# Attention and two MoE layers on one core: a planner that keeps VectorE's two-operand SBUF work and GpSimd's work apart

## The chip, the core and the metric

The kernel runs on one core of a Trainium2 chip. The metric is device time in microseconds (us) of one execution, the median of the runs shown. The core's engines are TensorE (PE in the rows, PEld for its weight loads), VectorE (DVE), ScalarE (ACT), GpSimd (POOL) and SyncE (SP, which issues the transfers). Each engine takes its instructions strictly in the order in which the program holds them. They wait for one another through semaphores.

## The reference

```python
def _attn_ref(q, k, v, tau):                  # q, k, v: (4, 8, 576, 64) fp32
    scores = np.matmul(q, k.transpose(0, 1, 3, 2)) / np.sqrt(64)
    thresh = np.max(scores, axis=-1, keepdims=True) - tau
    scores = np.where(scores >= thresh, scores, -1e9)
    attn = np.exp(scores - np.max(scores, axis=-1, keepdims=True))
    attn = attn / (np.sum(attn, axis=-1, keepdims=True) + 1e-9)
    return np.matmul(attn, v)
# x: (2304, 512); w_in: (512, 2048); w_out: (2048, 512)
def _moe_ref(x, w_in, w_out):
    h = x @ w_in
    return (h * np.tanh(softplus(h))) @ w_out
def _moe2_ref(x, w_in, w_out):
    h = x @ w_in
    return (h * np.clip(h + 3.0, 0.0, 6.0) / 6.0) @ w_out
# out = _moe2_ref(_moe_ref(attention, first pair of weights), second pair)
```

(`softplus` stands here for the reference's log1p form.)

## The kernel before

**Attention.** Heads are taken in 16 pairs. The 576 queries of a pair are four tiles of 128 and one of 64. Per pair, `k` and `q` are split into a high and a low fp32r part and `v` into two fp16 parts: ScalarE makes the high parts, VectorE the low parts of `k` (`kl`, line 982) and `v` (`vl`, line 1003), and GpSimd or VectorE the low part of `q` (`ql`). For a tile and a head the steps are: scores on TensorE into one of two PSUM buffers (`s`, line 1045), the row maximum on VectorE (`pk`, 1054), the exponential on ScalarE (`ex`, 1064), the threshold (`th`, 1059), the mask on VectorE (`mk`, 1067, the rows `e_ex<-s_s,...`), the fp16 high part on ScalarE (`ph`, 1072), the low part on GpSimd (`pl`, 317, two instructions `p_ph<-e_ex,p_ph`), a transposing transfer (`tr`), and the product with `v` on TensorE (`pv`, 1093). A score buffer is free again only when the mask has read it.

**Weights.** The four weight matrices arrive as 64-bit words, eight groups each. For a group VectorE takes a maximum (374) and some small scale instructions, ScalarE rescales the high words (490), GpSimd or VectorE shifts two halves left (`c`, 498 on GpSimd, 500 on VectorE), VectorE merges sign and low bits in two steps over 128x1024 words (506 and 511, called c3 and c4 here), ScalarE makes the fp16 high part (516), and GpSimd or VectorE the two halves of the low part (317, `w<-cvt_...`). After the eighth group a run of small VectorE instructions makes the scales (`zs`, 407 to 425). The first matrix is converted at the start of attention, the second at its end, the other two while the first dense layer runs.

**Dense layers.** The first product of the first layer (`h_g`, 648) is interleaved with attention. After attention come its activation and second product (`y_y`, 812), then the second layer (648 and 824), in which TensorE has nearly no idle time.

**What sets the order.** All of this is put into a `Plan` as tasks with a due time, engines that may take them with a cost each, dependencies and buffers. `Plan.run` goes forward with one clock per engine: of all open tasks it takes the one that can start first (within a small window per engine the one due first), puts its instructions at the end of that engine's queue, and moves that engine's clock by the cost. So costs and clocks decide the order on each engine, and at times the engine; on the chip only that order is left. In `_start` a task that GpSimd could take as well is started on VectorE 0.75 us late (`SLOW`). GpSimd's clock and VectorE's know nothing of each other.

Of the kernel before, what the change touches and what calls it, by code (L numbers as in the profile page):

```python
# [55 lines left out]
FLIP = 1.61  # L56
ALPHA = {"act": 3.07, "pe": 10.98}
FITS = 0.09
CRIT = ("s", "pk", "ex", "mk", "th")
BACKLOG = 99.0  # L60
MERGE_HI = False
# [67 lines left out]
class Plan:  # L129
# [10 lines left out]
    def __init__(self):  # L140
        self.clock = dict.fromkeys(("pe", "dve", "act", "pool", "sp"), 0.0)
        self.dma = 0.0
        self.warm, self.window, self.used = False, 1, 0.0
        self.open = {e: [] for e in self.clock}
        self.left = 0

# [25 lines left out]
    def _start(self, task, e):  # L172
        t = task.ready[e]
        for b in task.bufs:
            if b.slot is None:
                w = b.ring.when()
                if w is None:
                    return None
                t = max(t, w)
        if e == "sp" and not task.name.startswith("tr"):  # L180
            t = max(t + SLACK, self.dma - BACKLOG)
        if e == "dve" and len(task.engines) > 1:
            return max(t, self.clock[e]) + SLOW
        return max(t, self.clock[e])
# [43 lines left out]
    def run(self, until=None):  # L228
        while self.left and (until is None or any(t.end is None for t in until)):
# [18 lines left out]
            if e == "dve" and len(task.engines) > 1:  # L248
                start = max(start - SLOW, self.clock[e])
            cost = task.engines[e]  # L250
            if e == "pe":
                cost = self._clocked(start, cost, 0.75 if task.kind == "s" else 1.0)
            end = start + cost
            self.clock[e] = end
            if e == "sp":
                self.dma = max(self.dma, end + 1.1) + task.dma
                if task.kind == "tr":
                    self.clock[e] = max(end, self.dma - 0.95)
                end = self.dma + 1.1
            task.end = end  # L260
            task.fn(e)
            for b in task.bufs:
                b.drop(end)
            self.left -= 1
# [7 lines left out]
def fused_kernel(ctx: ExitStack, tc, q, k, v, tau, w1i, w1o, w2i, w2o, out):  # L272
# [125 lines left out]
    def summary(task, m, after):  # L398
# [25 lines left out]
            ts(w["c"][:, 0:1], w["c"][:, 0:1], 2.0 ** 10, None, ALU.mult)  # L424
            ts(w["f"], w["is"], w["c"][:, 1:2], None, ALU.mult)

        return task({"dve": 2.2 if n > 1 else 0.6}, scales, after, [], f"zs{m}")

    def tasker(at):
        def task(engines, fn, deps, bufs, tag, dma=0.0):  # L430
# [49 lines left out]
    def one_conversion(m, g, raw, deps, task):  # L480
# [37 lines left out]
        def lo(e, j):  # L518
            sub(e, dst[:, j, 1], t.tile[:, j].bitcast(F32), dst[:, j, 0])

        a = task(EXPAND, c1, deps, [raw, t], "c" + nm)
        b = [task(SHIFT, lambda e, j=j: c2(e, j), [a], [t], f"c{nm}{j}") for j in range(2)]
        a = task({"dve": 1.6}, c3, b, [raw, t], "c" + nm)
        a = task({"dve": 1.6}, c4, [a], [raw, t], "c" + nm)
        a = task({"act": 1.05}, hi, [a], [t], "h" + nm)
        for j in range(2):
            converted[m, 2 * g + j] = task(
                {"pool": 1.35, "dve": 0.68}, lambda e, j=j: lo(e, j), [a], [t], f"o{nm}{j}"
            )

    def split(task, name, src, sv, dst, inverse, ring, deps):
# [178 lines left out]
    def outer(ph, blk, x=None, ready=None):  # L710
# [30 lines left out]
        for fp in range(NG):  # L741
# [55 lines left out]
            a = chain["gs"] = task(  # L797
                {"act": 0.63}, hi, [a, scaled], [g, s], f"h{fp}", 0.0, fp, [chain["gs"]]
            )
            cost = {"dve": 0.75} if ph == 0 else {"pool": 1.35, "dve": 0.68}  # L800
            made.append(task(cost, lo, [a], [g, s], f"o{fp}", 0.0, fp))

        y = Buf(r_y)

# [153 lines left out]
    def pair(n, begin, values, sets):  # L958
# [4 lines left out]
        def prep(engines, fn, deps, bufs, tag, dma=0.0, at=early, order=()):  # L963
            return add(engines, fn, deps, bufs, at, 0.0, dma, f"{tag}{n}", order)
# [29 lines left out]
        a = prep({"act": 1.155}, lambda e: q_hi(slice(0, 2)), [lq], [rq, qs], "qh")  # L994
        for j in range(2):
            ql.append(prep(both(S), lambda e, j=j: q_lo(e, j), [a], [rq, qs], f"ql{j}_"))
        kl = prep({"dve": 1.8}, k_lo, [kh], [rk, kd, kld], "kl")

        def v_hi(e):
            nc.scalar.activation(vh.tile[:, :, :, :D], vb.tile, AF.Copy, scale=vs.tile)  # L1000
# [6 lines left out]
        def vprep(engines, fn, deps, bufs, tag):  # L1007
            return prep(engines, fn, [deps], bufs, tag, 0.0, base)

        a = vprep({"act": 0.83}, v_hi, scaled, [vb, vs, vh], "vh")  # L1010
        split = vprep({"dve": 1.3}, v_lo, a, [vb, vs, vh, vl], "vl")

        def query_tiles(t, c, o, i):
            at = START + t * STEP
# [246 lines left out]
    t = 0  # L1261
# [133 lines left out]
```

## Time and profile before

| | |
|---|---|
| median of 3 runs (1112.82 to 1121.19) | 1114.16 us |
| the profiled execution: its time, its span | 1116.12 us, 1114.3 us |
| busy: TensorE, VectorE, ScalarE, GpSimd | 980.6, 641.4, 610.2, 471.1 us |
| instructions: TensorE, VectorE, GpSimd | 8839, 1069, 397 |
| mean granted TensorE clock (share of 2.4 GHz) | 0.952 |

Times in rows are microseconds from the start of the span unless marked ns. A busy time runs from an instruction's start to its end, so that an instruction which started and was then held up by another engine counts as busy all that time. The rows of a line whose instructions do the same work show this: their shortest is the work, the rest is waiting inside the instruction.

### The profile page before, as it was taken

Reading aid. Unit: us, or ns where it says so; the run is one execution under the profiler, and the core shown is the slowest. Engines: PE = TensorE matmul, PEld = TensorE weight load, DVE = VectorE, ACT = ScalarE, POOL = GpSimd, SP = SyncE. Lnnn points to the kernel's source line nnn. Section 1 sums busy time; section 2 is a strip of 40 time slices with the busy share of each in tenths; the row PEclk is TensorE's granted clock in tenths of the full one; section 3 lists DMA queues with packets and bytes.
Section 4 is the critical chain, followed back from the end, with each engine's and each line's share of the span. In section 5 each row is a group of like instructions: output and inputs, shape, how many; then the busy total and the mean of one; then the engine's idle time right before and its main releaser. Section 6 shows DMA issues by size and latency. Waiting matters only on the chain. (4 is left out here: it accounts for less than half of the span.)

```text
span 1114.3 us, 21604 instructions
## 1 busy us (share of the span) xinstructions
PE 980.6 (88%) x8839; PEld 795.1 (71%) x8839; DVE 641.4 (58%) x1069; ACT 610.2 (55%) x992; POOL 471.1 (42%) x397
## 2 busy tenths in 40 slices
PE   2356698997999896879998999899999999999997
PEld 2256587986988785868887888787666666676663
DVE  7998998777777778767788788632111111111110
ACT  6565687886787776646665576632323323323322
POOL 4887665664565657543433045321212212212211
PEclk9977698997999996899999999999999999999999
DMA  8877379999799997765655986401100100100001
GB/s 274 211 211 189 86 208 239 193 238 232 155 217 194 199 218 166 164 236 214 228 191 196 346 309 239 141 21 38 39 11 29 38 12 28 39 16 24 19 1 38
DMA packets 199394, 162.87 MB, mean 146 GB/s; under 512 B 174080, under 2 KB 174080, under 8 KB 194176
## 3 DMA queue, kind: packets, MB, share of 16 engines
q1 hardware_dynamic: 199296, 161.51, 53.3%
q8 instruction: 69, 1.13, 0.4%
q14 instruction: 29, 0.24, 0.1%
HBM read 90.18 MB, written 28.84 MB: 107 GB/s over the span
## 5 line engine op out<-in xcount | busy, mean ns | idle before, releaser
L648 PEld LDWEIGHTS <-w 128*128 128x128 f16 x3456 | 335.0, 99 | 71.8 <-issue 10.6
L317 POOL TENSOR_TENSOR p_ph<-e_ex,p_ph 128x128 f16<-128x128 f32 (+3 forms) x160 | 194.4, 1236 | 128.0 <-ACT p_ph L1072 66.1
L317 POOL TENSOR_TENSOR gs_h<-hl_r,gs_h 128x512 f16<-128x512 f32 x72 | 83.2, 1156 | 302.1 <-ACT gs_h L787 302.1
L824 PE MATMUL y_y<-w,gs_h 128*128 128x512 f16 x864 | 201.2, 379 | 0.0
L812 PE MATMUL y_y<-gs_h,w 128*128 128x256 f16 x1728 | 192.3, 273 | 7.7 <-DVE yl_zhy L552 3.3
L648 PE MATMUL h_g<-x_fl,w 128*128 128x256 f16 x1536 | 189.5, 278 | 8.4 <-ACT he_t L696 6.4
L812 PEld LDWEIGHTS <-w 128*128 128x128 f16 x1728 | 168.3, 98 | 27.7 <-issue 8.2
L824 PEld LDWEIGHTS <-gs_h 128*128 128x128 f16 x864 | 84.5, 98 | 82.8
L787 ACT ACTIVATE gs_h<-hl_r 128x512 f16<-128x512 f32 x72 | 45.3, 629 | 159.1 <-PE y_y L824 155.3
L1054 DVE TENSOR_REDUCE nm_pk<-s_s 128x1 f32<-128x576 f32 x144 | 106.2, 752 | 40.7 <-PE s_s L1045 40.3
L1064 ACT ACTIVATE e_ex<-s_s,nm_pk 128x576 f32<-128x576 f32 x144 | 104.2, 731 | 29.9 <-DVE nm_pk L1054 25.1
L771 DVE SCALAR_TENSOR_TENSOR hl_r<-hl_r,f,hp_g 128x512 f32<-128x512 f32 x36 | 26.9, 747 | 161.8 <-ACT hl_r L765 161.8
L1067 DVE SCALAR_TENSOR_TENSOR e_ex<-s_s,thr_th,e_ex 128x576 f32<-128x576 f32 x144 | 111.6, 810 | 13.1 <-ACT thr_th L1059 10.6
L1093 PE MATMUL aux_pv<-vh,pt_tr 128*128 128x65 f16 (+1 forms) x1296 | 95.0, 212 | 18.8 <-DMA pt_tr<-p_ph 18.7
L1072 ACT ACTIVATE p_ph<-e_ex 128x576 f16<-128x576 f32 x144 | 95.7, 680 | 23.7 <-DVE e_ex L1067 22.0
L1045 PE MATMUL s_s<-kda_kh,qs 128*128 128x288 f32 x200 | 72.9, 377 | 39.8 <-DVE e_ex L1067 24.2
L1093 PEld LDWEIGHTS <-pt_tr 128*128 128x128 f16 x2016 | 88.9, 108 | 25.4 <-DMA pt_tr<-p_ph 23.4
L771 DVE SCALAR_TENSOR_TENSOR hl_r<-hl_r,f,h_g 128x512 f32<-128x512 f32 x36 | 26.9, 747 | 137.5 <-ACT hl_r L765 137.5
L648 PE MATMUL h_g<-xl_x,w 128*128 128x256 f16 x864 | 103.5, 273 | 0.0
L648 PE MATMUL hp_g<-xl_x,w 128*128 128x256 f16 x864 | 103.1, 273 | 0.0
L1045 PEld LDWEIGHTS s_s<-kda_kh,qs 128*128 128x128 f32 x200 | 46.1, 231 | 55.9 <-issue 29.6
L1045 PE MATMUL s_s<-klda_kl,qs 128*128 128x288 f32 x200 | 65.7, 341 | 0.0
(331 smaller groups left out, 1335.7 us busy)
## 6 DMA issues: line engine op xcount, KB each, us to landing
hd<-he_t SPq DMA_DIRECT2D x36, 512.0 KB, 3.7
hl_l<-hd SPq DMA_DIRECT2D x36, 512.0 KB, 5.1
raw_lr<-in_moe_w_in SPq DMA_DIRECT2D x16, 1024.0 KB, 5.9
raw_lr<-in_moe_w_out SPq DMA_DIRECT2D x16, 1024.0 KB, 7.2
rk_lk<-in_k SPq DMA_DIRECT2D x16, 576.0 KB, 4.9
rq_lq<-in_q SPq DMA_DIRECT2D x16, 576.0 KB, 5.9
raw_lw<-in_moe_w_out SPq DMA_DIRECT2D x8, 1024.0 KB, 7.3
v_lv<-in_v SPq DMA_DIRECT2D x16, 320.0 KB, 4.2
```

The costliest lines, as they stand in the source:

```text
L317: engine[e].tensor_tensor(dst, a, b, ALU.subtract)
L648: mm(hv[:, j, :], wj[:, wl, c * P : (c + 1) * P], x.tile[:, c, xl, :], start=j == 0 and n == 0, stop=j == 1 and n == 11, skip_group_check= ...
L771: nc.vector.scalar_tensor_tensor(half(g), half(g), wsc[2]["f"][:, fp : fp + 1], h.tile, ALU.min, ALU.mult)
L787: nc.scalar.activation(s.tile[:, 0], gv(), AF.Copy)
L812: mm(yv[:, h, :], wt[m2][f // 2][:, f % 2, wl, c * P : (c + 1) * P], gs[fp].tile[:, gl, f % 2, :], start=fp == 0 and n == 0, stop=fp == NG ...
L824: mm(y.tile[:, j], gs[fp].tile[:, gl, f % 2, j * P : (j + 1) * P], wt[m2][f // 2][:, f % 2, wl, :], start=fp == 0 and n == 0, stop=fp == N ...
L1045: mm(s[j].tile[:, half, :HALF], lh, rh[:, half * HALF : (half + 1) * HALF], start=m == 0, stop=m == len(terms) - 1,)
L1054: nc.vector.tensor_reduce(neg.tile[:, j : j + 1], sv(j), AX.XY, ALU.max, negate=True)
L1064: nc.scalar.activation(ev(j), sv(j), AF.Exp, bias=neg.tile[:, j : j + 1])
L1067: nc.vector.scalar_tensor_tensor(ev(j), sv(j), thr.tile[:, j : j + 1], ev(j), ALU.is_ge, ALU.mult)
L1072: nc.scalar.activation(p16.tile[:, js, :S], e_.tile[:, js], AF.Copy)
L1093: mm(ov[:, dst, :d], pt.tile[:, j, ch, :], part.tile[:, src, vc, :], start=i == j == ch == 0 and part is vh, stop=j == w - 1 and ch == 8, ...
```

## The change

The planner now makes two kinds of task exclude each other. A VectorE task whose kind is in `PORT` starts no earlier than GpSimd's clock, and a GpSimd task no earlier than the end of the last such VectorE task. The kinds are the low parts of `k`, `v`, `q` and of the weights, the shifts and merges of the weights, and the scale runs. The costs of these tasks, which were means with some waiting in them, become lower. A tag is renamed where the low part reads PSUM (`n`), so that it isn't in `PORT`, and where it belongs to a weight (`u`). `give` stays `None` everywhere, so `YIELD` is added nowhere. No instruction is given another form, and no semaphore is added: what changes is the order on each engine, and the engine of some halves.

```diff
+PORT = ("kl", "vl", "c", "ql", "u", "o", "zs")
+YIELD = 0.1
...
+        self.port, self.give = 0.0, None
...
+        if e == "dve" and task.kind in PORT:
+            t = max(t, self.clock["pool"])
+        if e == "pool":
+            t = max(t, self.port)
         if e == "dve" and len(task.engines) > 1:
             return max(t, self.clock[e]) + SLOW
...
             cost = task.engines[e]
+            if e == "pool" and self.give:
+                cost += YIELD
...
             self.clock[e] = end
+            if e == "dve" and task.kind in PORT:
+                self.port = end
...
             task.fn(e)
+            if e == "pool" and self.give:
+                self.give()
...
-        return task({"dve": 2.2 if n > 1 else 0.6}, scales, after, [], f"zs{m}")
+        return task({"dve": 1.6 if n > 1 else 0.6}, scales, after, [], f"zs{m}")
...
-        a = task({"dve": 1.6}, c3, b, [raw, t], "c" + nm)
-        a = task({"dve": 1.6}, c4, [a], [raw, t], "c" + nm)
+        a = task({"dve": 1.22}, c3, b, [raw, t], "c" + nm)
+        a = task({"dve": 1.22}, c4, [a], [raw, t], "c" + nm)
...
-                {"pool": 1.35, "dve": 0.68}, lambda e, j=j: lo(e, j), [a], [t], f"o{nm}{j}"
+                {"pool": 1.25, "dve": 0.68}, lambda e, j=j: lo(e, j), [a], [t], f"u{nm}{j}"
...
-            cost = {"dve": 0.75} if ph == 0 else {"pool": 1.35, "dve": 0.68}
-            made.append(task(cost, lo, [a], [g, s], f"o{fp}", 0.0, fp))
+            cost, tag = ({"dve": 0.75}, "n") if ph == 0 else ({"pool": 1.25, "dve": 0.68}, "o")
+            made.append(task(cost, lo, [a], [g, s], f"{tag}{fp}", 0.0, fp))
...
-        kl = prep({"dve": 1.8}, k_lo, [kh], [rk, kd, kld], "kl")
+        kl = prep({"dve": 1.42}, k_lo, [kh], [rk, kd, kld], "kl")
...
-        split = vprep({"dve": 1.3}, v_lo, a, [vb, vs, vh, vl], "vl")
+        split = vprep({"dve": 0.88}, v_lo, a, [vb, vs, vh, vl], "vl")
```

**Place one: VectorE in the first tiles, around a low part of `v` (`vlb_vl`).** Before, the fourth pair's stood between the row maxima (`nm_pk`) and both masks (`e_ex`) of a tile:

```order
L1054 TENSOR_REDUCE nm_pk_1_0_1_414<-s_s_1_1_0_375 128x1
L1164 TENSOR_SCALAR den_dt_0_2_429<-aux_pv_0_0_1_314 128x4
L1003 SCALAR_TENSOR_TENSOR vlb_vl_3_431<-v_lv_0_0_169,vs_ve_1_184,vh_140 128x640
L1067 SCALAR_TENSOR_TENSOR e_ex_1_0_2_421<-s_s_1_0_0_364,thr_th_1_0_1_433,e_ex_1_0_2_421 128x576
L1067 SCALAR_TENSOR_TENSOR e_ex_1_0_2_421<-s_s_1_1_0_375,thr_th_1_0_1_433,e_ex_1_0_2_421 128x576
L982 SCALAR_TENSOR_TENSOR kldb_kl_2_449<-rk_lk_0_369,qscale,kdb_kh_1_438 128x1152
L506 SCALAR_TENSOR_TENSOR cvt_c_1__1_424<-raw_lr_1_0_177,cvt_c_1__1_424 128x1024
```

Now the third pair's stands two tiles later than before, behind a merge (524 is the old 511) and ahead of the second row maximum of its tile:

```order
L1067 TENSOR_REDUCE nm_pk_0_0_1_446<-s_s_0_0_0_437 128x1
L524 SCALAR_TENSOR_TENSOR cvt_c_0__1_281<-raw_lr_0_0_175,cvt_c_0__1_281 128x1024
L1016 SCALAR_TENSOR_TENSOR vlb_vl_3_459<-v_lv_0_0_167,vs_ve_1_184,vh_136 128x640
L1067 TENSOR_REDUCE nm_pk_0_0_1_446<-s_s_0_1_0_448 128x1
L330 TENSOR_TENSOR x_fl_0_2_430<-aux_fl_0_1_429,x_fl_0_2_430 128x256
L1080 SCALAR_TENSOR_TENSOR e_ex_0_0_2_457<-s_s_0_0_0_437,thr_th_0_0_1_499,e_ex_0_0_2_457 128x576
L1080 SCALAR_TENSOR_TENSOR e_ex_0_0_2_457<-s_s_0_1_0_448,thr_th_0_0_1_499,e_ex_0_0_2_457 128x576
```

**Place two: VectorE between the twelfth and the thirteenth mask.** Before, no more than 16 instructions stood between two masks anywhere in the first conversion. The third group's merges stood like this:

```order
L1067 SCALAR_TENSOR_TENSOR e_ex_1_0_2_556<-s_s_1_1_0_508,thr_th_1_0_1_559,e_ex_1_0_2_556 128x576
L317 TENSOR_TENSOR x_fl_0_2_523<-aux_fl_0_1_522,x_fl_0_2_523 128x256
L506 SCALAR_TENSOR_TENSOR cvt_c_2__1_520<-raw_lr_2_0_416,cvt_c_2__1_520 128x1024
L385 TENSOR_SCALAR top_146<-top_146 128x1
L511 SCALAR_TENSOR_TENSOR cvt_c_2__1_520<-raw_lr_2_0_416,cvt_c_2__1_520 128x1024
L1054 TENSOR_REDUCE nm_pk_0_0_1_620<-s_s_0_0_0_599 128x1
```

Now 33 instructions stand between these two masks, and in their middle five that are in `PORT` follow one another:

```order
L330 TENSOR_TENSOR x_fl_0_2_430<-aux_fl_0_1_590,x_fl_0_2_430 128x256
L524 SCALAR_TENSOR_TENSOR cvt_c_1__1_412<-raw_lr_1_0_177,cvt_c_1__1_412 128x1024
L519 SCALAR_TENSOR_TENSOR cvt_c_2__1_588<-raw_lr_2_0_491,cvt_c_2__1_588 128x1024
L995 SCALAR_TENSOR_TENSOR kldb_kl_2_633<-rk_lk_0_375,qscale,kdb_kh_1_433 128x1152
L524 SCALAR_TENSOR_TENSOR cvt_c_2__1_588<-raw_lr_2_0_491,cvt_c_2__1_588 128x1024
L1016 SCALAR_TENSOR_TENSOR vlb_vl_3_671<-v_lv_0_0_169,vs_ve_1_184,vh_140 128x640
L1177 TENSOR_SCALAR den_dt_0_2_676<-aux_pv_0_0_1_593 128x4
L1067 TENSOR_REDUCE nm_pk_0_0_1_679<-s_s_0_0_0_666 128x1
```

Two groups' merges and the preparation of two pairs have moved together, with no mask between them.

**Place three: GpSimd in the conversion of the second matrix.** Before, one of the two shifts of the third and of the fourth group stood on VectorE, and GpSimd had the other:

```order
L498 TENSOR_TENSOR cvt_c_2__1_6586<-cvt_c_2__1_6586,eight 128x512
L317 TENSOR_TENSOR p_ph_4_0_1_6634<-e_ex_4_0_2_6604,p_ph_4_0_1_6634 128x64
L317 TENSOR_TENSOR p_ph_4_0_1_6634<-e_ex_4_0_2_6604,p_ph_4_0_1_6634 128x512
L317 TENSOR_TENSOR w_2_5416<-cvt_c_2__1_6586,w_2_5416 128x512 x2
L498 TENSOR_TENSOR cvt_c_3__1_6748<-cvt_c_3__1_6748,eight 128x512
L317 TENSOR_TENSOR w_3_5417<-cvt_c_3__1_6748,w_3_5417 128x512 x2
```

Now GpSimd has both halves (511 is the old 498), as of every group of every matrix:

```order
L330 TENSOR_TENSOR p_ph_4_0_1_6609<-e_ex_4_0_2_6584,p_ph_4_0_1_6609 128x64
L330 TENSOR_TENSOR p_ph_4_0_1_6609<-e_ex_4_0_2_6584,p_ph_4_0_1_6609 128x512
L511 TENSOR_TENSOR cvt_c_2__1_6635<-cvt_c_2__1_6635,eight 128x512 x2
L511 TENSOR_TENSOR cvt_c_3__1_6732<-cvt_c_3__1_6732,eight 128x512 x2
L330 TENSOR_TENSOR w_2_5431<-cvt_c_2__1_6635,w_2_5431 128x512 x2
L330 TENSOR_TENSOR w_3_5432<-cvt_c_3__1_6732,w_3_5432 128x512 x2
```

Six shifts and five low parts have moved in this way from VectorE to GpSimd in the whole program. In return VectorE takes six more of the evacuations that ScalarE shares with it (`he_t`), and four small normalisations of tail rows.

## Rows read from the trace of the kernel before

**Rows 1.** The page's first part: busy time of each engine, share, instructions.
```profile
PE 980.6 (88%) x8839; PEld 795.1 (71%) x8839; DVE 641.4 (58%) x1069; ACT 610.2 (55%) x992; POOL 471.1 (42%) x397
```
**Rows 2.** Windows: stretch, length, busy of PE, PEld, DVE, ACT, POOL, clock, DMA.
```profile
10.00:150.00 140.00, 78.97 (x687) 69.68 (x688) 128.78 (x196) 91.02 (x145) 105.01 (x80) 0.83 0.71 192
150.00:480.00 330.00, 290.29 (x3418) 262.27 (x3417) 258.14 (x438) 249.85 (x451) 191.19 (x159) 0.92 0.92 203
480.00:712.00 232.00, 214.71 (x1952) 190.62 (x1950) 184.29 (x320) 148.82 (x223) 90.18 (x71) 0.99 0.66 234
712.00:1115.00 403.00, 396.35 (x2786) 272.41 (x2785) 65.52 (x103) 118.07 (x174) 83.21 (x72) 1.00 0.09 30
```
**Rows 3.** Waits of PE, 0 to 712 us: total, times, longest.
```profile
PE s_s L1045 <- DVE e_ex L1067: 40.4, 22, 7.1
PE aux_pv L1093 <- DMA pt_tr<-p_ph: 18.7, 15, 2.5
PE h_zp L348 <- DVE he_t L698: 4.6, 1, 4.6
```
**Rows 4.** Timeline of DVE from 38.9 us: start, duration, instruction.
```profile
39.00 5.69 DVE L1003 SCALAR_TENSOR_TENSOR vlb_vl<-v_lv,vs_ve,vh 128x640 f16<-128x640 f32 x1
44.61 1.53 DVE L1067 SCALAR_TENSOR_TENSOR e_ex<-s_s,thr_th,e_ex 128x576 f32<-128x576 f32 x2
```
**Rows 5.** Timeline of POOL from 38 us.
```profile
38.28 2.51 POOL L317 TENSOR_TENSOR p_ph<-e_ex,p_ph 128x128 f16<-128x128 f32 x2
40.75 2.25 POOL L317 TENSOR_TENSOR w<-cvt_c__1_282,w 128x512 f16<-128x512 f32 x2
42.98 2.61 POOL L498 TENSOR_TENSOR cvt_c__1_424<-cvt_c__1_424,eight 128x512 int32<-128x512 int32 x2
```
**Rows 6.** Timeline of PE at 45 us, with the idle time before.
```profile
45.56 0.58 PE L1045 MATMUL s_s<-kdb_kh,qs 128*128 128x288 f32 x1 [7.13 <-DVE e_ex L1067]
```
**Rows 7.** Windows of line 1003 alone (`vl`): stretch, length, DVE busy, clock, DMA.
```profile
0.00:180.00 180.00, 18.02 (x8) 0.85 0.75 201
```
**Rows 8.** Line 1003 to 180 us: ns shortest/median/longest, first and last start.
```profile
L1003 DVE SCALAR_TENSOR_TENSOR vla_vl<-v_lv,vs_ve,vh x4: 873/1172/2234, 12.5 to 150.0; 128x640 f16<-128x640 f32 x4
```
**Rows 9.** Windows of line 982 alone (`kl`).
```profile
0.00:180.00 180.00, 13.97 (x8) 0.85 0.75 201
```
**Rows 10.** Line 982 to 180 us, as in Rows 8.
```profile
L982 DVE SCALAR_TENSOR_TENSOR klda_kl<-rk_lk,qscale,kda_kh x4: 1406/1418/2268, 10.5 to 136.5; 128x1152 fp32r<-128x1152 f32 x4
```
**Rows 11.** Windows of line 506 alone (c3).
```profile
0.00:180.00 180.00, 12.52 (x8) 0.85 0.75 201
```
**Rows 12.** Windows of line 511 alone (c4).
```profile
0.00:180.00 180.00, 15.19 (x8) 0.85 0.75 201
```
**Rows 13.** Line 511 to 180 us, one of its eight.
```profile
L511 DVE SCALAR_TENSOR_TENSOR cvt_c__1_802<-raw_lr,cvt_c__1_802 x1: 1211/1211/1211, 89.2 to 89.2; 128x1024 uint32<-128x1024 uint32 x1
```
**Rows 14.** Timeline of DVE from 123.5 us, the scale run (`zs`).
```profile
123.57 2.03 DVE L407 TENSOR_SCALAR s<-sc 128x8 f32<-128x8 f32 x1
125.63 5.54 DVE L408 TENSOR_SCALAR s<-s 128x8 uint32<-128x8 uint32 x1
131.21 0.17 DVE L409 TENSOR_SCALAR is<-s 128x8 uint32<-128x8 uint32 x1
```
**Rows 15.** Timeline of POOL, two places: a `ql`, and two shifts.
```profile
25.16 1.41 POOL L317 TENSOR_TENSOR qs<-rq_lq,qs 64x576 fp32r<-64x576 f32 x1
...
59.35 2.06 POOL L498 TENSOR_TENSOR cvt_c__1_520<-cvt_c__1_520,eight 128x512 int32<-128x512 int32 x2
```
**Rows 16.** Lines of DVE to 180 us: count, busy, mean ns, idle before.
```profile
L1054 DVE TENSOR_REDUCE nm_pk<-s_s 128x1 f32<-128x576 f32 x45 | 33.3, 747 | 4.3 <-PE s_s L1045 4.2
L1003 DVE SCALAR_TENSOR_TENSOR vlb_vl<-v_lv,vs_ve,vh 128x640 f16<-128x640 f32 x4 | 12.6, 3143 | 0.5 <-ACT vh L1000 0.5
L374 DVE TENSOR_REDUCE top<-raw_lr 128x1 f32<-128x1024 f32 x8 | 9.7, 1210 | 1.4 <-DMA raw_lr<-in_moe_w_in 1.4
```
**Rows 17.** Windows of line 500 alone (the shifts on VectorE).
```profile
0.00:712.00 712.00, 5.59 (x6) 0.93 0.79 212
```

## The prediction

> **What bounds the kernel now.** I read the page's first part, then the windows by stage, then TensorE's waits, and for the largest of these the timelines of the engines behind them. The first part says TensorE: 88% busy [rows 1]. The windows say where it is not. From 712 us to the end it works without a break, apart from some 6 us at the very end, so nothing that happens there on the other engines counts. From 480 to 712 us it idles 17 us, from 150 to 480 us 40 us, and from 10 to 150 us 61 of 140 us [rows 2]. The last is the stretch in which the first weight matrix is converted beside attention, and there VectorE is busy 129 of 140 us and GpSimd 105. So the front is VectorE's, and the reader should look at what its busy time consists of.
>
> TensorE's largest wait before 712 us is scores waiting for a mask, 40.4 us [rows 3]: there are two score buffers, and the mask frees them. The longest of these waits, 7.13 us, ends at 45.56 us [rows 6]. The mask before it started at 44.61 us, because a low part of `v` stood ahead of it and took 5.69 us [rows 4]; the same instruction takes 0.87 us when nothing holds it [rows 8]. Beside it GpSimd worked through a subtraction pair, two `w` halves and a shift, one after another, and its second shift was held in turn: 2.61 us for two that take 2.06 us elsewhere [rows 5, 15]. Two engines are shutting each other out here. VectorE did not get in after the instruction that was running, but only after several more.
>
> How much that is up to 180 us: the eight `vl` take 18.0 us for 8 x 0.87 = 7.0 [rows 7, 8]; the eight `kl` 14.0 for 8 x 1.41 = 11.2 [rows 9, 10]; c3 12.5 and c4 15.2 for 8 x 1.21 = 9.7 each [rows 11, 12, 13]; two steps of the scale run 7.6 for 2 x 0.17 [rows 14]. Held: 11.0 + 2.8 + 2.8 + 5.5 + 7.2 = 29 us of VectorE's time, in the stretch that VectorE bounds.
>
> **The change, part by part.** It doesn't lift the exclusion, it only lets the planner know of it. So the question is how much of the 29 us the new order avoids, and what it does instead.
>
> *What the front could give at most.* Count what both engines want from the shared resource between 10 and 150 us, at undisturbed durations. VectorE: 16 merges x 1.21, six `kl` x 1.41, five `vl` x 0.87 and a dozen scale steps x 0.17 = 34 us. GpSimd: 15 pairs of `pl` x 2.51 [rows 5], three smaller ones of about half that, 12 `ql` x 1.41, 16 shifts x 1.03 [rows 15], 16 `w` halves x 1.13 [rows 5] = 94 us. Together 128 of 140 us. No order of these instructions can save more than 12 us here. The 29 us that VectorE is held are mostly not waste: somebody else was using the resource.
>
> *Held time that the new order can avoid.* The 11.1 us of `kl`, c3 and c4 are mostly waits of one GpSimd instruction, and a plan that knows of them can put other VectorE work there. The 18.2 us of `vl` and the scale run come from GpSimd passing several times; the plan takes turns at such a place, and the chip did not [rows 4, 5]. Bounds: nothing, or the 12 us above. I take 10, close to the 11.1 us of the first sort.
>
> *The new run of 33 VectorE instructions between the twelfth and thirteenth mask.* Seven in it are of the exclusive kinds: five merges (6.1), a `kl` (1.4), a `vl` (0.9), 8.4 us. The rest are two maxima of weights at 1.21, two score maxima at 0.75 [rows 16], two of `v`, and some twenty small ones at 0.15 to 0.4: with the seven some 18 us. GpSimd's queue holds beside it five shifts, two `ql`, one `pl` pair and four `w` halves, 5 x 1.03 + 2 x 1.41 + 2.51 + 4 x 1.13 = 15 us, each group's merges waiting for its shifts. 8.4 + 15 is 23 us for 18 us of VectorE's work. For these no mask runs and no score buffer comes free, but VectorE's work is only moved, and it is what bounds the front. So I price the run at the difference, 5.5 us lost. The bounds are 0 (other VectorE work fits in) and some 12 (two of the seven wait as long as the row of 5.69 us).
>
> *150 to 480 us.* TensorE is 88% busy, and its waits there are mostly for transposing transfers (18.7 us over the whole stretch [rows 3]), which this order doesn't address. VectorE's exclusive work is thin, GpSimd 58% busy. Zero, with bounds of 4 each way, since every tile boundary is laid out anew.
>
> *480 to 712 us.* Eleven halves leave VectorE for GpSimd: some 12 us more there (1.03 and 1.13 each), which GpSimd at 90 of 232 us can hide [rows 2]; the six shifts alone cost VectorE 5.6 us [rows 17]. A group's two halves now follow each other, so its merges come a microsecond later; the cover is TensorE's queue of `h_g` work, and without it a microsecond for each of 11. Against this, the scale product `h_zp` of a late group, which held TensorE 4.6 us [rows 3], now has two full units of `h_g` ahead of the next one instead of a half. I take 1.5 us gained. From 712 us on the products fill TensorE: zero.
>
> *Sum.* -10 + 5.5 - 1.5 = -6 us against the profiled execution's 1116 us, so 1110 us. The median of the runs shown is 2 us below that execution: **1108 us**, 0.5% faster, which a measurement of this kernel can hardly tell from no change. I call everything within 1% of the median (11 us) the same.
>
> **A rule that says otherwise.** In the rows a waiting VectorE instruction was passed by four of GpSimd's that began after it [rows 4, 5]. The Trainium skill, "SBUF — State Buffer", section "Who interferes with whom", says that whoever issues first has the shared pair for its whole instruction and the other blocks until then; an operation of VectorE with two SBUF inputs counts against one of GpSimd that reads SBUF. By that rule, read as first come, first served, a wait would be one instruction of GpSimd, the planner's turns would be the chip's, and the time would be that of the first rival. The trace agrees on the exclusion, and differs on who is next: 5.69 us is longer than any single GpSimd instruction in it.
>
> **Rivals.**
> 1. *The turns work* (0.33). The new order puts the exclusive work where GpSimd pauses, and the front reaches what its 128 us of demand allow: -12 us; the 4.6 us wait for `h_zp` goes too, and the 150 to 480 us stretch gains some 2: -19 us from 1116, which on the scale of the runs' median is 1095 us (1086 to 1103). For it: the 29 us, and VectorE as the bound. Against it: the resource is 91% taken already, and the run of 33.
> 2. *GpSimd passes more often* (0.27), slower. A planned turn is no lock: a `vl` that is due between two GpSimd instructions stands at the head of VectorE's queue while GpSimd goes on. If all eight take the mean of the four `vlb`, 3.14 us [rows 16], they are held 18.2 us instead of 11.0, +7; the run of 33 costs its upper bound, +12; and of the 10 us saved elsewhere 6 are left: +13 us from 1116, on the median's scale 1127 us. It decides from about 40 us of VectorE held up to 180 us (now 29). For it: the row of 5.69 us. Against it: `vl` now stand in other places, some with GpSimd's queue waiting for ScalarE.
> 3. *It doesn't do what it says* (0.10). `give` is never set, so nothing on the chip holds GpSimd back, and the order is just another one: held time stays near 29 us, the time between 1108 and 1118 us, median 1114.
>
> My forecast has 0.30. With rival 3 that makes 0.40, of which I give 0.02 to its faster end: no change 0.38, faster by over 1% 0.35, slower by over 1% 0.27. The range that should hold the time 8 times in 10 leaves out the lower part of rival 1 and the upper part of rival 2: 1090 to 1131 us. The likeliest case alone spans 1103 to 1116 us.
>
> **What would show it.** For the forecast: VectorE's four lines above held some 20 us instead of 29 up to 180 us; one wait of TensorE of 10 us or more, for a mask, in the stretch from 55 to 85 us; the last merge of the first matrix within 5 us of where it was; the first unbroken product stretch some 6 us earlier than 712. For rival 1: held time under 12 us, and that stretch starting before 700. For rival 2: a `vl` of over 4 us with pairs of GpSimd beside it, held time over 40, the stretch starting after 722. The sum would be wrong if the order of tiles from 150 to 480 us, which I priced at zero, decided the time: then TensorE's idle time there would differ from 40 us by 10 or more, at a granted clock away from the 0.92 of that row.

## The result, and the profile after

The changed kernel takes 1088.3 us (median of four runs, 1086.8 to 1091.0) where the kernel before takes 1116.5: a ratio of 0.975, 95% interval 0.970 to 0.980, 2.5% faster. (The 1116.5 are of four runs; the first three of them have a median of 1114.2.) The forecast was 1108 us, with a range of 1090 to 1131.

The first part of the page of the changed kernel: busy time, share of the span, and instructions of each engine.

```profile
span 1087.7 us, 21597 instructions
...
PE 968.7 (89%) x8839; PEld 784.4 (72%) x8839; DVE 604.3 (56%) x1068; ACT 605.1 (56%) x982; POOL 469.2 (43%) x408
```

Against [rows 1] VectorE is the engine whose busy time fell most. The windows of [rows 2] in the changed kernel, the last two with their border moved with the shorter span:

```profile
10.00:150.00 140.00, 79.88 (x689) 68.25 (x690) 120.67 (x203) 92.44 (x149) 98.54 (x80) 0.76 0.69 182
150.00:480.00 330.00, 289.98 (x3525) 263.19 (x3522) 252.67 (x457) 250.95 (x448) 205.18 (x167) 0.97 0.99 220
480.00:690.00 210.00, 206.88 (x1889) 184.63 (x1888) 160.10 (x296) 141.93 (x215) 73.95 (x68) 0.99 0.71 246
690.00:1088.00 398.00, 391.68 (x2745) 268.23 (x2743) 66.27 (x102) 117.53 (x171) 90.01 (x78) 1.00 0.08 26
```

These rows are easily misread. From 10 to 150 us TensorE idles 60 us, as it did before, and from 150 to 480 us 40, also as before. But the same times no longer hold the same work, so fixed windows can't say where 27 us came from. Marks in the work itself can. VectorE has 144 mask instructions, nine for each pair of heads; the ends of the 48th and of the last are two such marks (`x2` in a row stands for two that follow each other, and the 48th is the second of them). First the kernel before (start, duration, instruction):

```profile
187.51 1.53 DVE L1067 SCALAR_TENSOR_TENSOR e_ex<-s_s,thr_th,e_ex 128x576 f32<-128x576 f32 x2
...
461.71 0.81 DVE L1067 SCALAR_TENSOR_TENSOR e_ex<-s_s,thr_th,e_ex 128x576 f32<-128x576 f32 x1
```

The same two in the changed kernel, where these lines' numbers are 13 higher:

```profile
183.16 1.54 DVE L1080 SCALAR_TENSOR_TENSOR e_ex<-s_s,thr_th,e_ex 128x576 f32<-128x576 f32 x2
...
444.10 0.81 DVE L1080 SCALAR_TENSOR_TENSOR e_ex<-s_s,thr_th,e_ex 128x576 f32<-128x576 f32 x1
```

They end at 189.0 and 462.5 us before, at 184.7 and 444.9 after; TensorE's last instruction ends at 1108.4 and 1081.7. So the **front** (to the 48th mask) gained 4.3 us, **attention** (48th to last) 13.3, and **the rest** 9.1: 26.7 together. Windows between the marks, before (length, busy of PE, PEld, DVE, ACT, POOL, granted clock, DMA):

```profile
0.00:189.00 189.00, 111.58 (x1083) 98.29 (x1084) 169.86 (x265) 125.68 (x206) 132.33 (x114) 0.86 0.77 203
189.00:462.50 273.50, 240.45 (x2815) 217.72 (x2813) 210.75 (x358) 207.67 (x376) 157.51 (x133) 0.91 0.91 196
462.50:760.00 297.50, 280.19 (x2592) 248.82 (x2591) 210.47 (x379) 174.68 (x261) 103.83 (x84) 0.99 0.61 209
```

and after:

```profile
0.00:184.70 184.70, 110.18 (x1055) 95.61 (x1056) 153.84 (x263) 122.57 (x199) 122.91 (x112) 0.82 0.77 194
184.70:444.90 260.20, 229.53 (x2834) 208.91 (x2832) 202.97 (x359) 204.52 (x373) 164.23 (x134) 0.97 1.01 216
444.90:760.00 315.10, 307.30 (x2790) 268.09 (x2788) 199.47 (x380) 181.46 (x269) 109.73 (x100) 0.99 0.57 197
```

Length less busy is TensorE's idle time. In attention it is 33.1 before and 30.7 after: only 2.4 of the 13.3 us. The other 10.9 are TensorE's busy time, 240.5 against 229.5 for the same tiles, at a granted clock of 0.91 against 0.97. It stood at the lower of its two levels (1.2 GHz) for 47.8 us before, in eight stretches, and for 17.1 us after, in five. TensorE's seven longest waits there took 2.2 to 2.6 us before and 1.6 to 2.3 after; that these made the difference in the clock is not shown. Behind attention the clock is 0.99 in both, and the idle time falls from 17.3 to 7.8 us, which is the whole gain there. In the front VectorE is busy 16.0 us less, but the front is only 4.3 us shorter: 11.7 us of that became VectorE's own idle time.

Who ended TensorE's waits from the last mask to 760 us (total, times, longest), before:

```profile
PE h_zp L348 <- DVE he_t L698: 4.6, 1, 4.6
PE y_y L812 <- DVE yl_zhy L552: 3.3, 1, 3.3
PE y_y L812 <- DVE gs_h L791: 3.1, 1, 3.1
PE h_g L648 <- ACT he_t L696: 1.8, 1, 1.8
```

and after, where nothing is left of the waits of `y_y`:

```profile
PE h_zp L361 <- DVE he_t L711: 4.3, 2, 3.1
PE h_zp L361 <- ACT he_t L709: 2.0, 1, 2.0
```

The held instructions. Line 1016 (`vl`) up to 190 us (length, DVE busy, clock, DMA), for [rows 7]; and the scale run, for [rows 14]:

```profile
0.00:190.00 190.00, 7.62 (x8) 0.82 0.78 198
```

```profile
130.75 0.18 DVE L420 TENSOR_SCALAR s<-sc 128x8 f32<-128x8 f32 x1
130.96 0.17 DVE L421 TENSOR_SCALAR s<-s 128x8 uint32<-128x8 uint32 x1
...
131.64 0.90 DVE L432 TENSOR_SCALAR b<-b 128x8 uint32<-128x8 uint32 x1
132.58 0.96 DVE L433 TENSOR_TENSOR b<-b,is 128x8 f32<-128x8 f32 x1
...
134.14 0.78 DVE L438 TENSOR_SCALAR f<-is,c 128x8 f32<-128x8 f32 x1
```

Of `vl`, 11.0 us of held time became 0.6; of the scale run 7.2 us vanished at the two steps shown before, and 2.1 came at three others (0.90, 0.96 and 0.78, against 0.17, 0.17 and 0.23). In the same window `kl` and c3 take 12.4 and 11.0 us, some 1.5 less each than in [rows 9, 11], and c4 takes 15.6, a little more than in [rows 12]. Held in the front: 29 us before, some 11 after.

### The profile page after: what moved, and what is told of

It is laid out like the page before. It is cut to its first block, busy times and chain, and to the rows that moved or that the text cites. A ratio compares the mean times of both kernels' runs of the same rounds, so it can differ in the third digit from the quotient of the medians.

```text
span 1087.7 us, 21597 instructions
## 1 busy us (share of the span) xinstructions
PE 968.7 (89%) x8839; PEld 784.4 (72%) x8839; DVE 604.3 (56%) x1068; ACT 605.1 (56%) x982; POOL 469.2 (43%) x408
## 3 DMA queue, kind: packets, MB, share of 16 engines
q8 instruction: 69, 1.13, 0.4%
## 4 chain that ended last, share of the span: by engine, by line
PE 71%; DMA 11%; DVE 8%; POOL 4%; ACT 3%; issue 2%; SPq 0%; ACTq 0%; POOLq 0%; DVEq 0%
PE h_g L661 19%; PE y_y L825 17%; PE y_y L837 17%; DMA pt_tr<-p_ph 9%; PE hp_g L661 9%; PE s_s L1058 4%; PE aux_pv L1106 4%; DVE e_ex L1080 2%; POOL p_ph L330 2%; DVE nm_pk L1067 1%; POOL qs L330 1%; DMA v_lv<-in_v 1%; ACT e_ex L1077 1%; DMA rq_lq<-in_q 1%; DMA raw_lr<-in_moe_w_in 1%
## 5 line engine op out<-in xcount | busy, mean ns | idle before, releaser
L825 PEld LDWEIGHTS <-w 128*128 128x128 f16 x1728 | 168.4, 98 | 19.3
L1080 DVE SCALAR_TENSOR_TENSOR e_ex<-s_s,thr_th,e_ex 128x576 f32<-128x576 f32 x144 | 111.6, 810 | 15.0 <-ACT thr_th L1072 11.1
L1106 PE MATMUL aux_pv<-vh,pt_tr 128*128 128x65 f16 (+1 forms) x1296 | 91.1, 207 | 29.8 <-DMA pt_tr<-p_ph 28.1
L1106 PEld LDWEIGHTS <-pt_tr 128*128 128x128 f16 x2016 | 83.8, 105 | 37.6 <-DMA pt_tr<-p_ph 33.3
L1085 ACT ACTIVATE p_ph<-e_ex 128x576 f16<-128x576 f32 x144 | 95.6, 680 | 25.7 <-DVE e_ex L1080 18.6
L1058 PE MATMUL s_s<-kda_kh,qs 128*128 128x288 f32 x200 | 68.5, 357 | 26.8 <-DVE e_ex L1080 18.3
L1058 PEld LDWEIGHTS s_s<-kda_kh,qs 128*128 128x128 f32 x200 | 43.2, 216 | 37.0 <-POOL qs L330 14.9
L804 DVE SCALAR_TENSOR_TENSOR gs_h<-hp_e,fscales,gs_h 128x512 f16<-128x512 f32 x72 | 52.6, 744 | 25.8 <-ACT gs_h L798 25.6
```

The costliest lines, as they stand in the source:

```text
L804: nc.vector.scalar_tensor_tensor(s.tile[:, 1], gv(), fs[:, fp : fp + 1], s.tile[:, 0], ALU.mult, ALU.subtract)
L825: mm(yv[:, h, :], wt[m2][f // 2][:, f % 2, wl, c * P : (c + 1) * P], gs[fp].tile[:, gl, f % 2, :], start=fp == 0 and n == 0, stop=fp == NG ...
L1058: mm(s[j].tile[:, half, :HALF], lh, rh[:, half * HALF : (half + 1) * HALF], start=m == 0, stop=m == len(terms) - 1,)
L1080: nc.vector.scalar_tensor_tensor(ev(j), sv(j), thr.tile[:, j : j + 1], ev(j), ALU.is_ge, ALU.mult)
L1085: nc.scalar.activation(p16.tile[:, js, :S], e_.tile[:, js], AF.Copy)
L1106: mm(ov[:, dst, :d], pt.tile[:, j, ch, :], part.tile[:, src, vc, :], start=i == j == ch == 0 and part is vh, stop=j == w - 1 and ch == 8, ...
```

## The experiments

*Rules* are here the two exclusions of the plan, *prices* the six lowered costs. Three theories stood at the start. *Holding*: the gain is held time avoided in the front, carried to the end. *Behind the front*: rules or prices pay in attention and behind it. *Scatter*: the planner decides between near-equal tasks, any disturbance makes another order, and the order before was a poor one.

All ratios are to the kernel before, on the same chip. A switch lets the plan change its mind at a time of its own clock (185 us there is about the 48th mask on the chip):

```diff
+    def new(self):
+        return NEW_FROM <= self.clock["dve"] < NEW_TO
+    def cost(self, task, e):
+        c = task.engines[e]
+        return c if self.new() else OLD.get((task.kind, c), c)
...
-        if e == "dve" and task.kind in PORT:
+        if e == "dve" and task.kind in PORT and self.new():
...
-        if e == "pool":
+        if e == "pool" and self.new():
```

**Prices alone.**

```diff
-PORT = ("kl", "vl", "c", "ql", "u", "o", "zs")
+PORT = ()
```

> The new prices of the tasks alone, without the two rules that make VectorE's two-operand instructions and GpSimd's wait for each other in the plan. If the rules are what gained: VectorE's four exclusive lines are held some 25 to 30 us up to 180 us again (29 before, 36 less 18 in the changed kernel), and the time is 1108 to 1118 us. If the prices are what gained (shorter prices put the merges and low parts earlier): 1088 to 1096 us. If neither, and any new order scatters by itself: anything from 1085 to 1125, with no relation to the held time.

1095.2 us, ratio 0.979 (0.976 to 0.983). The prices alone are faster, with VectorE held 49 us in the whole program (60 before).

**Rules alone.** The six prices set back, in this manner:

```diff
-        a = task({"dve": 1.22}, c3, b, [raw, t], "c" + nm)
+        a = task({"dve": 1.6}, c3, b, [raw, t], "c" + nm)
...
```

> The two rules with the old prices. If the rules are what gained: vl held under 3 us and the scale run under 2 us up to 180 us, and 1086 to 1096 us. If the prices are: 1108 to 1118 us. If orders scatter by themselves: anything from 1085 to 1125.

1100.1 us, 0.986 (0.983 to 0.989). VectorE is held 17 us and GpSimd 13, less than in the changed kernel (22 and 19), and yet it is slower than that and than the prices alone: held time and run time do not go together.

**Front alone, and the rest alone.** `NEW_FROM, NEW_TO = 0, 185` and `185, 9e9`.

> The changed kernel's plan (rules and prices) up to 185 us of the plan's own time, and from there the plan of the kernel before. If the front carries the gain, because less time held there leaves later stages earlier: 1088 to 1098 us. If the stages behind 185 us carry it (the 48th mask was only 4.3 us earlier in the changed kernel, the last 17.6): 1106 to 1114 us. If orders scatter by themselves: 1085 to 1125.

1102.8 us, 0.987 (0.984 to 0.990), between the theories.

> The plan of the kernel before up to 185 us of the plan's time, with its row of 5.69 us and its order unchanged there, and the changed kernel's plan from there. If the front carries the gain: 1108 to 1116 us. If the stages behind it do: the 48th mask where it was (189 us), the last one 10 to 15 us earlier than 462, and 1088 to 1100 us. If orders scatter by themselves: 1085 to 1125, and the sum of this kernel's gain and that of the one with the front alone is not 28 us.

1095.4 us, 0.980 (0.977 to 0.983). The 48th mask ends at 188.0, the last at 445.8. With the 5.69 us stall left in place, most of the gain is there: *holding* in the front as the whole cause has fallen. But the two gains add to 37 us, not 28, as *scatter* said they would.

**Is the order before a poor draw?** Prices off by up to 1% from 185 us of the plan's time on, by a hash of the task's name, and neither rules nor new prices. The digit ahead of the name makes another draw of the same noise:

```diff
+        if self.clock["dve"] < 185:
+            return c
+        return c * (1.0 + 0.01 * (2.0 * (zlib.crc32(f"1{task.name}{e}".encode()) % 1000) / 999.0 - 1.0))
```

> A control: the kernel before with its old prices and without the two rules, but from 185 us of the plan's time each task's price is changed by up to 1% either way, by a hash of its name. Up to there the order is that of the kernel before. If the rules and prices are what gained behind 185 us (22 us with them from there on): within 6 us of 1117. If the order of the kernel before was a poor draw among orders that the planner holds for equal, so that nearly any other is better: 1092 to 1106 us, with VectorE and GpSimd still held as long as before (60 and 33 us in all).

1097.8 us, 0.982 (0.980 to 0.984), with the front's stalls still there (55 and 32 us held in all).

> The same control with another hash. If the rules and prices gained: within 6 us of 1117. If the order before was a poor draw: 1092 to 1106 us. If orders simply scatter to both sides: the two controls differ from each other by more than 8 us, one of them above 1117.

1106.3 us, 0.990 (0.988 to 0.991). Two orders that mean nothing gave 19 and 11 us.

**The moved halves alone.** `SHIFT = {"pool": 1.0}` in the kernel before.

> The kernel before with the shifts of a conversion allowed on GpSimd alone (six of them were on VectorE, from about 500 us on); no rule, no new price. If moving work from VectorE to GpSimd behind attention is what gained there: the start of the second product of the first layer stays near 523 us, the last merge of the fourth matrix comes 5 to 8 us before 708, and the time is 1106 to 1111 us. If it is not: 1113 to 1120 us.

1122.5 us, 1.004 (1.002 to 1.007): no part of the gain.

**Late part alone.** `NEW_FROM, NEW_TO = 400, 9e9`.

> The kernel before up to 400 us of the plan's time (some 420 us on the chip), and the rules and prices from there. In the kernel with both from 185 us the last mask came 16.7 us earlier and the end 19. If the gain arises along attention, from 190 to 420 us, and is only carried on: 1107 to 1113 us. If it arises in attention's last 40 us and behind it (before, TensorE idles 13 us from 420 to 480 and 17 us from 480 to 712): 1093 to 1102 us.

1104.4 us, 0.988 (0.985 to 0.991), between the two: the last mask at 457.1, and 12.4 us of TensorE idle from it to 760 us.

**The same noise on the changed kernel.** If that were just a good draw, noise would spoil it.

> The changed kernel (rules and new prices throughout), with each task's price off by up to 1% from 185 us of the plan's time on, by the same hash as the first control of the kernel before, which took 1097.8 us. If the rules and prices have a worth of their own behind 185 us: 1080 to 1090 us, 10 us or more below that control. If they are worth only what the front gains (4.3 us at the 48th mask): 1090 to 1098. If the changed kernel was itself a lucky draw: above 1096.

1091.8 us, 0.978 (0.973 to 0.982): within what the front alone would leave.

> The changed kernel with the second hash; the kernel before with it took 1106.3 us. If rules and prices have a worth of their own behind 185 us: 1082 to 1092 us. If only the front's 4.3 us: 1096 to 1106.

1087.7 us, 0.974 (0.970 to 0.978).

> The changed kernel with a third hash. With a worth of their own: 1080 to 1092 us, and 12 us or more below the kernel before with this hash. With the front alone: 1092 to 1106 and some 4 us below it.

1087.2 us, 0.974 (0.970 to 0.978).

> The kernel before with the third hash from 185 us of the plan's time on. If the order before was a poor draw: 1092 to 1108 us again, now three of three below it. If orders scatter to both sides of it: above 1112.

1118.7 us, 1.001 (0.998 to 1.005). So the orders without rules and new prices scatter over 21 us, from 1097.8 to 1118.7, with the kernel before near the slow end; four orders with rules and prices lie within 5 us, all faster than any without. *Scatter* explains part of the 28 us, not the rest.

**What held time is worth.** In the order before, the low part of `v` by an instruction that isn't held:

```diff
-            nc.vector.scalar_tensor_tensor(
-                vl.tile, vb.tile, vs.tile, vh.tile[:, :, :, :D], ALU.mult, ALU.subtract
-            )
+            nc.vector.tensor_reduce(
+                vl.tile, vb.tile.rearrange("p a c (d o) -> p a c d o", o=1), AX.X, ALU.max
+            )
```

> The kernel before in its own order, with the low part of v made by an instruction of the same size with one input (a maximum over groups of one element), which in the trace before is never held; this leaves the subtraction out, so the low part is not the low part. If VectorE's held time of some 10 us on these instructions up to 180 us is what the changed kernel gained in the front: the 48th mask some 3 to 5 us earlier than 189 us, and that much or less at the end (1112 to 1117 us against 1117). If held time converts fully: the 48th mask 8 to 11 us earlier and 1106 to 1110. If GpSimd was held off by nothing and simply shifts: no change.

1114.4 us, 0.997 (0.995 to 1.000). The line's instructions to 180 us (shortest, median, longest ns, first and last start), and the 48th mask:

```profile
L1003 DVE TENSOR_REDUCE vla_vl<-v_lv x4: 807/807/815, 12.2 to 148.1; 128x640 f16<-128x640 f32 x4
L1003 DVE TENSOR_REDUCE vlb_vl<-v_lv x4: 793/808/810, 27.1 to 169.8; 128x640 f16<-128x640 f32 x4
```

```profile
183.66 1.53 DVE L1067 SCALAR_TENSOR_TENSOR e_ex<-s_s,thr_th,e_ex 128x576 f32<-128x576 f32 x2
```

None is held: the eight take 6.5 us instead of 18.0 [rows 7]. The window to the 48th mask:

```profile
0.00:185.20 185.20, 110.69 (x1079) 97.95 (x1080) 160.96 (x265) 124.52 (x206) 131.95 (x114) 0.85 0.77 206
```

So 11.6 us less on this line is 8.9 less on VectorE (161.0 against 169.9 for the same 265 instructions): the others took 2.7 us longer. The mask came 3.8 us earlier than in the trace before (185.2), and 2.9 earlier than the mean of the seven traces with that order (below). The end came about 3 us earlier (0.6 to 5.4 by the interval). Of the time taken off the held line, a quarter to a third became time at the mark.

**Prices or rules, at other draws.** The same noise on each alone.

> New prices without the rules, with the second hash from 185 us of the plan's time (with neither: 1106.3 us; with both: 1087.7). The first kernel with prices alone took 1095.2. If the prices carry most of what is gained behind 185 us: 1088 to 1098 us. If rules and prices are both needed: 1098 to 1106.

1108.8 us, 0.993 (0.990 to 0.995).

> The rules with the old prices, second hash (neither: 1106.3, both: 1087.7). The first kernel with the rules alone took 1100.1, with the least held time of all. If less held time is what gains behind 185 us: 1086 to 1094 us. If the prices are: 1098 to 1106, with the front's 4 us.

1108.8 us, 0.992 (0.989 to 0.995), with 16 and 12 us held.

> New prices without the rules, third hash (neither: 1118.7 us, both: 1087.2). If prices and rules gain only together, since the prices leave out the held time that the rules add: 1095 to 1112 us, with 5 us or more of TensorE idle behind 480 us. If the second hash was a poor draw for the prices and they carry the gain: 1086 to 1095.

1105.1 us, 0.990 (0.987 to 0.992).

> The rules with the old prices, third hash (neither: 1118.7 us, both: 1087.2). If rules and prices gain only together, since the old prices hold the held time that the rules count again: 1096 to 1112 us, with VectorE held under 20 us in all and yet 8 us or more of TensorE idle behind 480 us. If less held time is the gain: 1086 to 1095.

1103.3 us, 0.988 (0.985 to 0.991), with 19 and 10 us held.

**Prices nearer still**, all in the changed kernel:

```diff
-SHIFT = {"pool": 1.0, "dve": 0.6}
+SHIFT = {"pool": 1.04, "dve": 0.93}
...
-        return task({"dve": 1.3}, top, [loaded], [raw], "zw" + name)
+        return task({"dve": 1.22}, top, [loaded], [raw], "zw" + name)
...
```

> The changed kernel with five more prices moved to what the trace shows (maxima of weights 1.30 to 1.22, halves on GpSimd 1.25 to 1.16, shifts 1.00 to 1.04 there and 0.60 to 0.93 on VectorE, maxima of the second layer's input 1.15 to 1.22, thresholds 0.20 to 0.29). If prices nearer to the chip's are what gains, and more of them gain more: 1078 to 1085 us. If the gain is used up: 1085 to 1093, as the changed kernel and its three controls.

1089.3 us, 0.976 (0.972 to 0.979), where the changed kernel is: the gain is used up. No version tried is faster than the changed kernel by more than the noise.

**All draws together.** The first draw is without noise; the other two are the second and third hash. Lengths in us as above; "lost to the clock" is TensorE's busy time times one less its granted clock, summed over attention; idle is TensorE's from the last mask to 760 us; held is what VectorE's and GpSimd's instructions took beyond the shortest of their line and shape, good to some 3 us, since it depends on how small an excess is counted.

| | median us | 48th mask | attention | lost to the clock | idle behind | held |
|---|---|---|---|---|---|---|
| neither | 1116.5, 1106.3, 1118.7 | 189.0, 188.5, 188.3 | 273.5, 266.4, 273.4 | 19.3, 10.8, 13.7 | 17.3, 14.9, 18.6 | 60+33, 54+29, 49+36 |
| prices | 1095.2, 1108.8, 1105.1 | 187.9, 187.1, 186.6 | 262.9, 262.1, 265.0 | 8.9, 15.3, 12.6 | 13.7, 18.1, 15.3 | 49+29, 53+34, 47+31 |
| rules | 1100.1, 1108.8, 1103.3 | 184.5, 185.2, 184.4 | 264.5, 269.5, 267.2 | 12.8, 14.0, 13.8 | 12.5, 17.1, 15.2 | 17+13, 16+12, 19+10 |
| both | 1088.3, 1087.7, 1087.2 | 184.7, 184.7, 183.1 | 260.2, 263.6, 263.0 | 7.9, 8.9, 11.9 | 7.8, 6.2, 6.0 | 22+19, 24+19, 22+15 |

Seven traces have VectorE's order of the kernel before up to the 48th mask (what was changed in six of them comes later); it ends at 187.0 to 189.0 us in these, at 188.1 in the mean. Five have the changed kernel's: 182.9 to 184.7, mean 183.9. So the front's 4 us are clear of that spread, and they come with the rules, at every draw; what the prices alone bring there, 0 to 1.5 us, is hardly clear of it. Attention is some 8 us shorter with prices alone and 9 with both; but the control with the first hash, which is not in the table since the single parts were not run with it, had 256.6 us without either, so that difference is not beyond scatter. Behind attention neither part alone changes the idle time beyond scatter, and with both throughout it falls from 12 to 19 us to 6 to 8 (9.9 and 8.2 in the two other such kernels). The windows from the last mask to 760 us at the third hash, neither:

```profile
461.60:760.00 298.40, 279.78 (x2564) 247.39 (x2562) 194.08 (x364) 170.32 (x255) 92.01 (x74) 0.98 0.58 200
```

prices, rules, and both:

```profile
451.60:760.00 308.40, 293.13 (x2667) 256.96 (x2666) 202.37 (x377) 173.87 (x261) 91.34 (x76) 0.98 0.58 196
```

```profile
451.60:760.00 308.40, 293.16 (x2655) 256.27 (x2652) 195.61 (x375) 176.77 (x267) 107.35 (x99) 0.98 0.60 203
```

```profile
446.10:760.00 313.90, 307.94 (x2799) 268.12 (x2797) 199.14 (x387) 185.60 (x278) 110.77 (x101) 1.00 0.58 202
```

Length less the first number is 18.6, 15.3, 15.2 and 6.0. What TensorE waited for with the rules alone:

```profile
PE h_g L677 <- DVE top L414: 5.3, 2, 4.9
PE y_y L841 <- DVE gs_h L820: 4.3, 2, 3.0
```

With VectorE held only 19 us in the whole kernel, TensorE still waits for it. Ahead of the longest of these waits, which ended at 490.63 us, VectorE stood idle 3.81 us at a weight's maximum, because the weight's transfer had not landed, and the small step that TensorE needed was queued behind it:

```profile
489.16 1.22 DVE L403 TENSOR_REDUCE top<-raw_lr 128x1 f32<-128x1024 f32 x1 [3.81 <-DMA raw_lr<-in_moe_w_out]
490.29 0.28 DVE L380 TENSOR_REDUCE top<-h_zp 128x1 f32<-128x128 f32 x1
490.49 0.14 DVE L414 TENSOR_SCALAR top<-top 128x1 uint32<-128x1 uint32 x1
```

The longest wait behind attention in the kernel before, 4.6 us for the `he_t` at 484.91 us, has the same cause:

```profile
483.41 1.22 DVE L374 TENSOR_REDUCE top<-raw_lr 128x1 f32<-128x1024 f32 x1 [7.10 <-DMA raw_lr<-in_moe_w_out]
484.67 0.15 DVE L385 TENSOR_SCALAR top<-top 128x1 uint32<-128x1 uint32 x1
484.91 0.75 DVE L698 TENSOR_SCALAR he_t<-h_g,hin 128x512 f32<-128x512 f32 x1
```

No instruction in these rows is held. These two waits are a matter of order alone: a maximum stood in VectorE's queue ahead of its data, and ahead of what TensorE needed. No run moved it by itself.

A reading that fits: the old prices contain held time, so with the rules the plan counts it twice, and the new prices without the rules leave it out, and only both together come near the durations in the trace. That is argued, not shown, and something speaks against it: the two kernels with both from 185 or from 400 us on idle 12.0 and 12.4 us there, hardly less than the best with one part, 12.5.

So **shown** is: 4 us from the rules at the 48th mask; order scatter of up to 21 us behind it; and a gain from rules and prices together beyond that scatter, since all five kernels with both throughout (1087.2 to 1091.8) have lower medians than all fourteen others tried and the one before. With the same draw on both sides (no noise, then the three hashes) the gains are 28, 6, 19 and 31 us: with the first hash little more than the front's 4. **Open** is how that gain splits between the parts. The means over the three draws are 1113.8, 1103.0, 1104.0 and 1087.7: -10.8 and -9.8 alone and -26.1 together. That is 5.5 us more than the sum, with draws of one kind up to 14 us apart, so whether the parts only add up is open too. Which of the kinds in `PORT` matters was not tried.

## Why the prediction was wrong

- **The term that failed is "150 to 480 us. Zero, with bounds of 4 each way", and with it "480 to 712 us ... 1.5 us gained".** Attention behind the 48th mask gave 13.3 us, 10.9 of them TensorE's busy time at a higher granted clock, and the rest 9.1, all of them TensorE's idle time. (The marks lie near the prediction's borders, not on them.) The wait for `h_zp` that the 1.5 us were to come from stayed, 4.6 us before and 4.3 and 2.0 after; those of `y_y` went. The zero rested on transposing transfers being what TensorE waits for there and on thin exclusive work, so that exclusion could not matter. But the change also gives the planner other prices, and a planner fed with other numbers lays out every tile anew. The prediction said just that, as a reason for a bound of 4 us; in the controls 1% of noise moved the end by 19 and 11 us forward, and by 2 back, which is within the noise of the measurement. It had not asked how far from a typical order the order before was.
- **The front's net was right by luck: -10 + 5.5 = -4.5 us forecast, 4.3 measured; both of its terms were off.** "The 18.2 us of `vl` and the scale run" were held not to be avoidable; 15 of them were avoided, while the 11.1 us said to be avoidable went down to 8.3. But time saved is not held time avoided: 16.0 us less busy time of VectorE gave 4.3, and 8.9 us less in the run with the other instruction 3.8. The ceiling of 12 us stood (13, since GpSimd's items add up to 93 us and not 94). Of the **run of 33 instructions** the order was as described and the price wasn't: the 13th mask ended at 80.2 us instead of 67.5, but the 30th at 126.8 instead of 136.5. The forecast wait of 10 us did not come. The longest from 53 to 86 us (total, times, longest):

```profile
PE aux_pv L1106 <- DMA pt_tr<-p_ph: 4.6, 2, 4.4
PE aux_fl L1221 <- DVE top L398: 4.2, 1, 4.2
```

- **The first rival came near the time (1095 us, 1086 to 1103) and not by its own sum.** Its sign of under 12 us held came true (11). But it put 12 of its 19 us in the front, where 4 arose, and 2 in the stretch to 480 us, where half did. The page cited there (the Trainium skill, "SBUF — State Buffer", section "Who interferes with whom"), read as first come, first served, has a loser wait for the running instruction only; the changed kernel's trace agrees in the place shown at the end, and the row of 5.69 us [rows 4] does not.
- **The second rival's condition, 40 us of VectorE held, did not arise.** The reason against it held: the `vl` stand elsewhere now. **The third**, just another order, was given 0.10 with a time of 1108 to 1118 us. Its first half is partly what happened; its band was far too narrow, since orders without rules and new prices lie from 1097.8 to 1122.5.
- **The tests.** The first matrix' last merge ends at 144 us (142 before), as forecast. The unbroken product stretch begins not 6 us before 712, but at 483.6, behind TensorE's last wait of over a microsecond. The test for the zero, TensorE's idle time from 150 to 480 us differing from 40, could not see its own failure: it was 40.0 again, with 3525 recorded matmuls in place of 3418 and the clock at 0.97 for 0.92.

## What to carry to other kernels

Where a planner sets the order, a change of its prices or rules is a new draw of the whole program: before asking what the change avoids, disturb the old order with a per cent of noise and see how far that alone moves the time. Here it moved it by up to 19 us, and only the same noise on both sides showed that rules and prices together gain beyond it. And measure stages between marks in the work (the 48th mask, the last mask), not between times, since a stretch that holds more work looks unchanged.

## What the runs showed of the hardware

Who comes next when VectorE and GpSimd exclude each other differs from place to place. In the kernel before, one `vl` was passed by three GpSimd instructions that began after it, two `w` halves and a shift [rows 4, 5]; the prediction counts four, but the second shift was itself held. In the changed kernel, VectorE at 61 to 69 us:

```profile
61.44 1.55 DVE L524 SCALAR_TENSOR_TENSOR cvt_c__1_412<-raw_lr,cvt_c__1_412 128x1024 uint32<-128x1024 uint32 x1
63.93 1.23 DVE L519 SCALAR_TENSOR_TENSOR cvt_c__1_588<-raw_lr,cvt_c__1_588 128x1024 uint32<-128x1024 uint32 x1 [0.94 <-POOL cvt_c__1_588 L511]
65.07 2.31 DVE L995 SCALAR_TENSOR_TENSOR kldb_kl<-rk_lk,qscale,kdb_kh 128x1152 fp32r<-128x1152 f32 x1
67.30 2.18 DVE L524 SCALAR_TENSOR_TENSOR cvt_c__1_588<-raw_lr,cvt_c__1_588 128x1024 uint32<-128x1024 uint32 x1
```

and GpSimd in the same stretch:

```profile
60.87 3.02 POOL L511 TENSOR_TENSOR cvt_c__1_588<-cvt_c__1_588,eight 128x512 int32<-128x512 int32 x2 [3.32 <-ACT cvt_c__1_588 L503]
64.22 4.18 POOL L330 TENSOR_TENSOR w<-cvt_c__1_412,w 128x512 f16<-128x512 f32 x2 [0.33 <-ACT w L529]
```

Here they take strict turns: the two halves take 4.18 us (2 x 1.13 when free), each having let one VectorE instruction by, and the `kl` 2.31 (1.41 when free), having let one half by. What decides between turns and being passed is open.

A one-input maximum of the size of `vl` took 793 to 815 ns in all eight places where the two-input form took up to 5.69 us. The Trainium skill, "SBUF — State Buffer", section "Who interferes with whom", says that such a maximum never contends on this chip; the trace agrees.
